# Moving the last head group's rows in five chunk-sized groups instead of eight pairs, with a turned ring and new orders

## Chip, cores and metric

One core of one Trainium2 chip runs the kernel. The metric is the device time of one execution in microseconds (us).

## The reference

Four layers in a row over x of 2048 tokens and 448 features: attention, MLP, attention, MLP (the same weights twice), each with a layernorm without weights and a residual. Attention is local and dilated: 16 heads of 28, and a token looks at 8 keys, 2 tokens apart.

```python
    def _A_ref(x, wqkv, wo):
        B, S, D = x.shape
        H = 16; Dh = D // H
        W, dil = 8, 2
        ...
        logits = jnp.einsum("bhsd,bhswd->bhsw", q, kg) * scale
        logits = jnp.where(mask[None, None, :, :], logits, -1e9)
        attn = _softmax(logits, axis=-1)
        o = jnp.einsum("bhsw,bhswd->bhsd", attn, vg)
        return (lambda x, *d: x.transpose(*d))(o, 0, 2, 1, 3).reshape(B, S, D) @ wo

    def _B_ref(x, w_gate, w_up, w_down):
        g = jnp.einsum("bsd,df->bsf", x, w_gate)
        u = jnp.einsum("bsd,df->bsf", x, w_up)
        h = g * u
        return jnp.einsum("bsf,fd->bsd", h, w_down)
    ...
    x = x + _A_ref(_layernorm(x, axis=-1), A_wqkv, A_wo)
    x = x + _B_ref(_layernorm(x, axis=-1), B_w_gate, B_w_up, B_w_down)
    x = x + _A_ref(_layernorm(x, axis=-1), A_wqkv, A_wo)
    x = x + _B_ref(_layernorm(x, axis=-1), B_w_gate, B_w_up, B_w_down)
```

## The kernel before, in words

**Blocks and chunks.** The 2048 tokens are 16 blocks of 128 (0 to 15). The layers are numbered 0 to 3; 0 and 2 are attention, 1 and 3 the MLP. They are worked off in chunks that interleave: the chunks of layer 2 are 512 tokens each, those of layer 3 are 256, 512, 512, 512 and 256 tokens, that is blocks 0 to 1, 2 to 5, 6 to 9, 10 to 13 and 14 to 15.

**Matmuls.** Nearly all whole matmuls are issued by a helper at L352, in pairs on the upper and lower half of TensorE's rows. The same products can be issued at L355 as four strips of 32 columns, which stand between the small matmuls of an attention burst (scores at L837, probabilities times values, AV, at L872) and fill TensorE there.

**Attention.** Queries and keys are cast out of PSUM (qk, L714, on ScalarE or VectorE as the order says); the keys' rows that hold the values are written to a DRAM tensor vt (L723), and come back transposed as v_sb (L734). In this way AV needs a transposed load. The results are copied to O_sb (L886, L890). `norm` divides them by the sums of the probabilities: a shuffle (L900), Ln and Exp on ScalarE (L901, L902) and a VectorE multiply (L913), which writes the bf16 values to the ring oT. The ring holds 8 blocks, 1024 tokens (`HALF`), so a multiply whose tokens cross token 1024 is cut in two there.

**Output projection.** `y_blocks` makes the projection of two blocks. A head has 28 rows in a group of 32, so 4 rows in each group are free. In layer 2 (`FOLD`) the last four heads' rows are moved into these free rows, and 7 pairs of matmuls do instead of 8. That takes five moves for each two blocks on SyncE's DMA queue (SP): four of them (`mv`, by the table `PADS`) wait for the norms of the two blocks; the fifth (`mw`) waits for the four and shifts what is left of the odd block to the other half of the partitions. The matmuls of both blocks wait for the fifth. All five are plain DMAs of L445. The rows of the weights wo_g are moved in the same manner once (`wf`), after the last projection of layer 0.

**Order.** Nothing decides the order at run time. A table `ORDER` gives for each engine and for SP the numbers of the operations in their order, with burst entries that say which strips stand between which small matmuls; `BANKS` gives the PSUM banks. Waits on semaphores are put in from the dependences. An instruction that waits holds up all that stands behind it on its engine, and a DMA issue that waits holds up all DMAs behind it on SP.

**MLP.** For 14 slices of 128 features, gate and up matmuls (a unit, 14 matmuls for each), ScalarE's copy g_sb (L979), VectorE's multiply hT (L982), then the down projection with WD. The last two blocks are done by full-width matmuls (L994) with the addition at L998. All other projections are added to x_sb on VectorE (L943).

Of the kernel before, what the change touches and what calls it, by code (L numbers as in the profile page):

```python
# [7 lines left out]
S = 2048  # L8
D = 448
# [24 lines left out]
FOLD = {0: 16, 2: 0}  # L34
PADS = ((0, 64, 4, 14, 0), (1, 96, 4, 15, 0), (2, 80, 3, 14, 16), (3, 112, 3, 15, 16))
# [61 lines left out]
def grp_nc(g):  # L97
# [283 lines left out]
def build(nc, A_x, A_wqkv, A_wo, B_w_gate, B_w_up, B_w_down, out):  # L381
# [513 lines left out]
    def norm(li, g, qb, os_, prio):  # L895
# [15 lines left out]
        for a, z in zip(cut, cut[1:]):  # L911
            def fn(E, a=a, z=z):
                return E.tensor_tensor(oT[:, :, a % HALF:a % HALF + z - a], O[:, :, a - tok:z - tok], R_sb[:, rs, 0:w].rearrange("p (h n) -> p h n", h=4)[:, :, a - tok:z - tok], ALU.mult)  # L913
# [211 lines left out]
```

## Time and profile before

| what | value |
|---|---|
| median of 3 runs | 383.45 us (383.18 to 383.95) |
| profiled execution | 383.47 us, its span 381.7 us |
| granted TensorE clock | 1.0 |
| TensorE (PE) busy | 373.9 us, 98% |
| VectorE (DVE) busy | 288.1 us, 75% |
| ScalarE (ACT) busy | 198.0 us, 52% |
| GpSimd (POOL) busy | 7.8 us, 2% |

A row of the timeline gives start and length in us, the engine, the line, the operation, what it writes and reads, how many instructions are grouped, and in brackets the idle time before it with the releaser that the semaphores suggest. SPq is SyncE's DMA queue: the length there is that of the issue, not of the transfer. A row of the waits gives total us, times, and the longest one. A row of the windows gives the length of the stretch, then busy time and instructions of PE, PEld (weight load), DVE, ACT and POOL, the granted clock, the DMA share and GB/s.

### The profile page before, as it was taken

What the parts mean: (1) busy time and instruction counts of PE and PEld (TensorE: products, weight loads), DVE (VectorE), ACT (ScalarE), POOL (GpSimd) and SP (SyncE); (2) the same over time, 40 slices, a digit from 0 to 9 for tenths busy, and PEclk for the clock granted to TensorE, in tenths of its full rate; (3) what the DMA queues carried; (4) which work ended last, traced back from release to release, by engine and by line L of the source; (5) the groups of instructions that cost most, each with busy time, mean ns of one, the idle gap of its engine ahead of it and who ended that gap; (6) DMA issues with size and microseconds to landing.
All of it is one profiled execution on the core that took longest, in us unless ns stands there. A gap on an engine that the chain in (4) does not pass through costs nothing.

```text
span 381.7 us, 14424 instructions
## 1 busy us (share of the span) xinstructions
PE 373.9 (98%) x6388; PEld 209.8 (55%) x6388; DVE 288.1 (75%) x649; ACT 198.0 (52%) x379; POOL 7.8 (2%) x36
## 2 busy tenths in 40 slices
PE   7999999999999999999999999999989999999997
PEld 3645577654554445444676666555555544444864
DVE  7988999989759794968568977758887878266423
ACT  5798896766516355245645326628745633034410
POOL 7000000000000000000000000000000000000000
PEclk9999999999999999999999999999999999999999
DMA  7665543500130215332102221630124001502003
GB/s 262 165 158 147 96 127 81 97 7 3 26 78 16 43 25 72 43 43 44 34 18 27 45 50 29 106 47 6 25 43 76 9 19 29 122 17 47 2 2 120
DMA packets 56209, 22.97 MB, mean 60 GB/s; under 512 B 45812, under 2 KB 56132, under 8 KB 56148
## 3 DMA queue, kind: packets, MB, share of 16 engines
q1 hardware_dynamic: 56004, 22.00, 27.5%
q8 instruction: 50, 0.82, 0.9%
q14 instruction: 11, 0.09, 0.1%
q10 hardware_dynamic: 144, 0.06, 0.1%
HBM read 8.59 MB, written 2.71 MB: 30 GB/s over the span
## 4 chain that ended last, share of the span: by engine, by line
PE 91%; DVE 4%; ACT 2%; DMA 1%; issue 1%; SPq 0%; DVEq 0%
PE ps L352 82%; PE ps L355 4%; PE ps L837 2%; PE ps L872 2%; PE ps L994 1%; ACT qk L714 1%; DMA v_sb<-vt 1%; DVE xn_sb L604 1%; DVE st L583 1%; DMA x_sb<-in_A_x_dram 1%; DVE v_sb L806 0%; DVE WQK L522 0%; DVE hT L982 0%; DVE Qz L825 0%; DVE xnTa L628 0%
## 5 line engine op out<-in xcount | busy, mean ns | idle before, releaser
L352 PE MATMUL ps<-xnTb,WGU 64*128 64x512 bf16 (+1 forms) x1890 | 171.2, 332 | 0.3 <-DVE qk L714 0.3
L352 PEld LDWEIGHTS ps<-xnTb,WGU 64*128 64x128 bf16 x1890 | 92.3, 94 | 70.6 <-issue 1.6
L979 ACT ACTIVATE g_sb<-ps 128x512 bf16<-128x512 f32 (+1 forms) x140 | 69.3, 510 | 83.9 <-PE ps L352 72.0
L982 DVE TENSOR_TENSOR hT<-g_sb,ps 128x512 bf16<-128x512 bf16 (+1 forms) x140 | 78.0, 574 | 36.3 <-ACT g_sb L979 35.5
L352 PE MATMUL ps<-WD,hT 64*128 64x448 bf16 x794 | 81.3, 349 | 0.0
L352 PEld LDWEIGHTS ps<-WD,hT 64*128 64x128 bf16 x794 | 38.3, 94 | 33.3 <-ACT E_sb L847 0.4
L943 DVE TENSOR_TENSOR x_sb<-x_sb,ps 128x448 bf16<-128x448 bf16 x62 | 37.1, 613 | 21.6 <-PE ps L352 21.3
L352 PE MATMUL ps<-xnTa,WQK 64*128 64x512 bf16 (+1 forms) x490 | 51.8, 352 | 0.3 <-DVE WQK L522 0.2
L847 ACT ACTIVATE E_sb<-ps,shift_sb 128x1024 bf16<-128x1024 f32 (+1 forms) x36 | 37.5, 1072 | 12.0 <-PE ps L837 11.9
L583 DVE BATCH_NORM_STATS2 st<-x_sb 128x6 f32<-128x448 bf16 x64 | 38.3, 613 | 1.0 <-DMA x_sb<-in_A_x_dram 0.8
L604 DVE TENSOR_SCALAR xn_sb<-x_sb,mv,rstd 128x512 bf16<-128x512 bf16 (+1 forms) x64 | 35.4, 574 | 2.5 <-ACT rstd L588 2.0
L352 PEld LDWEIGHTS ps<-xnTa,WQK 64*128 64x128 bf16 x490 | 23.0, 94 | 20.7 <-DVE O_sb L890 0.4
L714 ACT ACTIVATE qk<-ps 128x1024 bf16<-128x1024 f32 (+1 forms) x29 | 26.6, 931 | 11.4 <-PE ps L352 6.3
L901 ACT ACTIVATE R_sb<-R_sb 128x480 f32<-128x480 f32 (+1 forms) x34 | 20.4, 604 | 17.2 <-DVE R_sb L900 17.0
L854 DVE TENSOR_TENSOR E_sb<-E_sb,MK 128x1024 bf16<-128x1024 bf16 (+1 forms) x36 | 23.5, 656 | 6.6 <-ACT E_sb L847 6.6
L352 PE MATMUL ps<-wo_g,oT 64*128 64x448 bf16 x236 | 27.1, 349 | 1.1 <-DVE hT L982 1.1
L913 DVE TENSOR_TENSOR oT<-O_sb,R_sb 128x480 bf16<-128x480 f32 (+3 forms) x36 | 21.9, 626 | 3.8 <-ACT R_sb L902 3.6
L352 PE MATMUL ps<-WV,xnTa 64*128 64x336 bf16 (+3 forms) x248 | 23.2, 304 | 0.5 <-DVE O_sb L890 0.5
L900 DVE STREAM_SHUFFLE R_sb<-O_sb 128x480 f32<-128x480 f32 (+1 forms) x34 | 23.1, 692 | 0.0
L586 ACT ACTIVATE lnv<-mv,eps_sb 128x2 f32<-128x2 f32 (+2 forms) x31 | 9.0, 295 | 25.9 <-DVE mv L585 24.0
L902 ACT ACTIVATE R_sb<-R_sb 128x480 f32<-128x480 f32 (+1 forms) x34 | 20.0, 607 | 0.3
L886 ACT ACTIVATE O_sb<-ps 128x512 f32<-128x512 f32 (+1 forms) x20 | 10.9, 570 | 15.8 <-PE ps L872 15.8
(66 smaller groups left out, 223.8 us busy)
## 6 DMA issues: line engine op xcount, KB each, us to landing
out_dram<-x_sb SPq DMA_DIRECT2D x15, 112.0 KB, 1.8
x_sb<-in_A_x_dram SPq DMA_DIRECT2D x3, 448.0 KB, 5.3
hT<-in_A_wqkv_dram SPq DMA_DIRECT2D x4, 224.0 KB, 4.4
WGU<-in_B_w_gate_dram SPq DMA_DIRECT2D x4, 224.0 KB, 3.9
WGU<-in_B_w_up_dram SPq DMA_DIRECT2D x4, 224.0 KB, 4.5
WD<-in_B_w_down_dram SPq DMA_DIRECT2D x2, 448.0 KB, 3.8
WGU<-in_B_w_gate_dram SPq DMA_DIRECT2D x2, 336.0 KB, 4.5
WGU<-in_B_w_up_dram SPq DMA_DIRECT2D x2, 336.0 KB, 4.8
```

Source lines behind the costliest of these rows:

```text
L352: return lambda E: E.matmul(out(), lhs(), rhs(), start=start, stop=stop)
L583: sc.add("dve", one(lambda E, B=B: E.bn_stats(st6[:, B, :], x_sb[:, B, :]), ("bn", li, B)), 525.0, deps=[("x", li - 1, B)] + ([("xn", li - ...
L604: sc.add("dve", one(lambda E, B=B, dst=dst, src=src: E.tensor_scalar(dst, src, mv[:, B, 0:1], rstd[:, B:B + 1], ALU.subtract, ALU.mult), ( ...
L714: return E.activation(dst, src, ACT.Copy) if hasattr(E, "activation") else E.tensor_copy(dst, src)
L847: return E.activation(E_sb[:, slot, 2 * hp:2 * hp + 2, 0:w], ps[:, b0:b0 + 2, 0:w], ACT.Exp, bias=shift_sb[:, 0:1], scale=SCALE)
L854: return E.tensor_tensor(e, e, MK[:, kind, 0:nc].unsqueeze(1).unsqueeze(1).to_broadcast([128, 2, w // nc, nc]), ALU.min)
L900: sc.add("dve", one(lambda E: E.stream_shuffle(R_sb[:, rs, 0:w], O_sb[:, os_, 0:w], [DH] * 32), ("Rs", li, qb)), dve_est(w) + 20.0, deps=[ ...
L901: sc.add("act", one(lambda E: E.activation(R_sb[:, rs, 0:w], R_sb[:, rs, 0:w], ACT.Ln), ("Rl", li, qb)), act_est(w, False), deps=[("Rs", l ...
L913: return E.tensor_tensor(oT[:, :, a % HALF:a % HALF + z - a], O[:, :, a - tok:z - tok], R_sb[:, rs, 0:w].rearrange("p (h n) -> p h n", h=4 ...
L943: sc.add("dve", one(lambda E: E.tensor_tensor(x_sb[:, B, :], x_sb[:, B, :], ps[:, bk[w], 0:D], ALU.add), ("x", li, B)), dve_est(D), deps=[ ...
L979: sc.add("act", one(lambda E, gs=gs, bk=bk: E.activation(g_sb[:, gs, 0:nt], ps[:, bk[0], 0:nt], ACT.Copy), ("G", li, j, fc)), act_est(nt), ...
L982: sc.add("dve", one(lambda E, gs=gs, bk=bk, fc=fc: E.tensor_tensor(hT[:, fc, hs, 0:nt], g_sb[:, gs, 0:nt], ps[:, bk[1], 0:nt], ALU.mult), ...
```

## The change

The moves are made once for each chunk of layer 3's MLP: `GROUPS` names the first blocks 0, 2, 6, 10 and 14. The four `mv` of a group wait for the norms of all its 2 or 4 blocks, and each projection of the group waits for the group's one `mw`. That makes 25 moves instead of 40; those of four blocks are 512 tokens wide instead of 256. For a group to lie in one piece in the ring, the ring is turned by 256 tokens: block B stands at place (B + 2) % 8 instead of B % 8, and norms are cut at tokens 768 and 1792 instead of 1024. The orders and banks of all engines are written anew.

```diff
+GROUPS = (0, 2, 6, 10, 14)
...
-        cut = [tok] + [HALF] * (tok < HALF < tok + nq) + [tok + nq]
+        cut = [tok] + [e for e in range(HALF - 256, S, HALF) if tok < e < tok + nq] + [tok + nq]
...
-        nd = []
-        for qb in range(NQB):
-            _, _, tok, nq = qb_info(qb)
-            if tok < 128 * (B + 2) and tok + nq > 128 * B:
-                nd.append(("N", li, qb))
+        def norms(b0, b1):
+            return [("N", li, qb) for qb in range(NQB) if qb_info(qb)[2] < 128 * b1 and qb_info(qb)[2] + qb_info(qb)[3] > 128 * b0]
+        nd = norms(B, B + 2)
         fold = B >= FOLD[li]
         if fold:
-            a = 128 * (B % 8)
-            for j, row, m, _, _ in PADS:
-                plain_dma("sp", oT[32 * j + DH:32 * j + 32, 0:m, a:a + 256], oT[row:row + 4 * m, 3, a:a + 256], ("mv", li, B, j), ...
-            plain_dma("sp", oT[64:128, 3, a + 128:a + 256], oT[0:64, 3, a + 128:a + 256], ("mw", li, B), ...
-            nd = nd + [("mw", li, B)]
+            G = max(g for g in GROUPS if g <= B)
+            n = min([g for g in GROUPS if g > B] + [NBLK]) - G
+            if B == G:
+                a = 128 * ((B + 2) % 8)
+                for j, row, m, _, _ in PADS:
+                    plain_dma("sp", oT[32 * j + DH:32 * j + 32, 0:m, a:a + 128 * n], oT[row:row + 4 * m, 3, a:a + 128 * n], ("mv", li, B, j), ...
+                odd = [oT[lo:lo + 64, 3, a:a + 128 * n].rearrange("p (b w) -> p b w", w=256)[:, :, 128:256] for lo in (64, 0)]
+                plain_dma("sp", odd[0], odd[1], ("mw", li, B), ...
+            nd = nd + [("mw", li, G)]
...
 ORDER = {
     "sp": (
...
-        "841 847 763 765 772 776 917 819 777 915 919 921 1016 1018 816 817 815 814 935 820 821 934 822 938 939 936 818 823 937 940 945 944 950 949 1076 1074 973 "
+        "763 841 765 845 819 776 820 772 915 777 917 919 921 944 1013 1011 939 821 936 940 938 937 815 934 822 816 823 817 935 814 818 1164 945 950 949 1071 "
```

What the new orders do is seen at three places.

**SP, the moves of blocks 6 to 9.** Here `oT<-oT 4x4x…` and `4x3x…` are the four `mv`, `64x128` or `64x2x128` the `mw`, and `vt<-qk` the writes of keys and values of the last chunk of layer 2. Before, from the `mw` of blocks 6 and 7 on:

```order
L445 DMA oT<-oT 64x128
L723 DMA vt<-qk 4x4x512 x5
L445 DMA oT<-oT 4x4x256
L445 DMA oT<-oT 4x3x256
L445 DMA oT<-oT 4x4x256
L445 DMA oT<-oT 4x3x256
L734 DMA_TRANSPOSE v_sb<-vt 128x128
L723 DMA vt<-qk 4x4x512 x2
L445 DMA oT<-oT 64x128
```

After:

```order
L723 DMA vt<-qk 4x4x512 x4
L445 DMA oT<-oT 4x4x512
L445 DMA oT<-oT 4x3x512 x2
L445 DMA oT<-oT 4x4x512
L723 DMA vt<-qk 4x4x512 x3
L445 DMA oT<-oT 64x2x128
L734 DMA_TRANSPOSE v_sb<-vt 128x128 x3
```

Ten moves in two sets have become five in one; between `mv` and `mw` stand three writes of vt, where a transposed load and two writes stood.

**TensorE, the projections of blocks 6 to 9.** Matmuls with wo_g and oT are the projection, WV those of the values, xnTb with WGU gate and up. Before, behind the score burst of 17 small rows that the projection's first eight matmuls precede:

```order
L352 MATMUL ps<-wo_g,oT 128x448 x6
L352 MATMUL ps<-WV,xnTa 128x336 x6
L352 MATMUL ps<-xnTb,WGU 128x512 x14
L352 MATMUL ps<-WV,xnTa 128x336 x14
L352 MATMUL ps<-wo_g,oT 128x448 x8
L352 MATMUL ps<-WV,xnTa 128x336 x8
L352 MATMUL ps<-wo_g,oT 128x448 x6
```

After, from the end of the gate and up strips of the burst before (the score burst of 17 rows left out):

```order
L352 MATMUL ps<-xnTb,WGU 128x512 x20
L352 MATMUL ps<-WV,xnTa 128x336 x6
L352 MATMUL ps<-xnTb,WGU 128x512 x14
L352 MATMUL ps<-WV,xnTa 128x336 x22
...
L352 MATMUL ps<-wo_g,oT 128x448 x28
L352 MATMUL ps<-xnTb,WGU 128x512 x18
```

The projections of blocks 6 to 9 stand together, and all 28 matmuls of WV and a score burst stand ahead of them.

**SP, the transposed loads of the first bursts of layer 2.** `wo_g<-in_A_wo_dram` is a `wf`, which waits for the last projection of layer 0. Before:

```order
L723 DMA vt<-qk 4x4x512 x2
L734 DMA_TRANSPOSE v_sb<-vt 128x128 x2
L607 DMA_TRANSPOSE xnTa<-xn_sb 128x4x128
L445 DMA wo_g<-in_A_wo_dram 4x1792
L734 DMA_TRANSPOSE v_sb<-vt 128x128
L607 DMA_TRANSPOSE xnTa<-xn_sb 128x4x128 x3
```

After:

```order
L445 DMA wo_g<-in_A_wo_dram 4x1792
L734 DMA_TRANSPOSE v_sb<-vt 128x128
L445 DMA wo_g<-in_A_wo_dram 4x1792
L734 DMA_TRANSPOSE v_sb<-vt 128x128
L607 DMA_TRANSPOSE xnTa<-xn_sb 128x4x128
L734 DMA_TRANSPOSE v_sb<-vt 128x128
```

All three loads stand behind a `wf` now, the last of them behind two and one transpose of xn_sb.

More of the change, by code (lines that the diff above doesn't have):

```diff
@@ L918, in y_blocks @@
         bk = Banks(2)
-        nd = []
-        for qb in range(NQB):
-            _, _, tok, nq = qb_info(qb)
-            if tok < 128 * (B + 2) and tok + nq > 128 * B:
-                nd.append(("N", li, qb))
+        def norms(b0, b1):
+            return [("N", li, qb) for qb in range(NQB) if qb_info(qb)[2] < 128 * b1 and qb_info(qb)[2] + qb_info(qb)[3] > 128 * b0]
+        nd = norms(B, B + 2)
         fold = B >= FOLD[li]
         if fold:
-            a = 128 * (B % 8)
-            for j, row, m, _, _ in PADS:
-                plain_dma("sp", oT[32 * j + DH:32 * j + 32, 0:m, a:a + 256], oT[row:row + 4 * m, 3, a:a + 256], ("mv", li, B, j), f"d_m{li}_{B}", deps=nd, prio=prio - 0.1)
-            plain_dma("sp", oT[64:128, 3, a + 128:a + 256], oT[0:64, 3, a + 128:a + 256], ("mw", li, B), f"d_m{li}_{B}", deps=[("mv", li, B, j) for j in range(4)], prio=prio - 0.1, mode=1)
-            nd = nd + [("mw", li, B)]
+            G = max(g for g in GROUPS if g <= B)
[3 more added lines that the diff above has]
+                for j, row, m, _, _ in PADS:
+                    plain_dma("sp", oT[32 * j + DH:32 * j + 32, 0:m, a:a + 128 * n], oT[row:row + 4 * m, 3, a:a + 128 * n], ("mv", li, B, j), f"d_m{li}_{B}", deps=norms(B, B + n), prio=prio - 0.1)
+                odd = [oT[lo:lo + 64, 3, a:a + 128 * n].rearrange("p (b w) -> p b w", w=256)[:, :, 128:256] for lo in (64, 0)]
+                plain_dma("sp", odd[0], odd[1], ("mw", li, B), f"d_m{li}_{B}", deps=[("mv", li, B, j) for j in range(4)], prio=prio - 0.1, mode=1)
+            nd = nd + [("mw", li, G)]
             if B == FOLD[li] and li == min(l for l in FOLD if FOLD[l] < NBLK):
```

6 lines of the change are left out of this document (3 added, 3 removed), and 129 rows, old and new, of tables (BANKS, ORDER).

## The prediction

> **What bounds the kernel now.** I read the page first (busy shares, the slices with the granted clock, the chain that ended last), then TensorE's waits, the timeline about each wait that the change can touch, and the windows for the stretch where VectorE is fullest.
>
> ```profile
> PE 373.9 (98%) x6388; PEld 209.8 (55%) x6388; DVE 288.1 (75%) x649; ACT 198.0 (52%) x379; POOL 7.8 (2%) x36
> PEclk9999999999999999999999999999999999999999
> PE 91%; DVE 4%; ACT 2%; DMA 1%; issue 1%; SPq 0%; DVEq 0%
> ```
>
> TensorE is busy for 373.9 of 381.7 us at full granted clock, and the chain runs through it for 91%. So the time is TensorE's work plus its gaps, 7.8 us. The matmul work does not change: the groups in the order of both kernels hold the same products, and where strips take the place of whole matmuls, four strips replace one. I therefore ask only which gaps close and which open. TensorE's waits, longest first:
>
> ```profile
> PE ps L514 <- DVE hT L475: 1.3, 1, 1.3
> PE ps L352 <- DVE hT L982: 1.1, 1, 1.1
> ...
> PE ps L872 <- DMA v_sb<-vt: 0.5, 1, 0.5
> PE ps L352 <- DVE O_sb L890: 0.5, 1, 0.5
> PE ps L352 <- DVE qk L714: 0.3, 1, 0.3
> ```
>
> The first belongs to the head, whose loads the change leaves alone. The second is the one that the moves can touch. About it, in this order: whole matmuls of L352 from 258 to 280 us by operand (minimum, median and maximum in ns, first and last start), SyncE's issues, VectorE, and the two TensorE rows about the wait:
>
> ```profile
> L352 PE MATMUL ps<-xnTb,WGU x104: 373/376/387, 258.2 to 275.7; 64*128 64x512 bf16 x104
> L352 PE MATMUL ps<-xnTa,WQK x28: 376/376/376, 261.2 to 264.0; 64*128 64x512 bf16 x28
> L352 PE MATMUL ps<-wo_g,oT x28: 346/349/361, 272.3 to 280.0; 64*128 64x448 bf16 x28
> L352 PE MATMUL ps<-WV,xnTa x28: 302/303/303, 274.0 to 279.5; 64*128 64x336 bf16 x28
> ```
>
> ```profile
> 269.97 2.69 SPq L445 DMA_DIRECT2D oT<-oT  x4
> 272.70 1.12 SPq L734 DMA_TRANSPOSE v_sb<-vt  x1
> 273.87 0.82 SPq L723 DMA_DIRECT2D vt<-qk  x2
> 274.73 0.54 SPq L445 DMA_DIRECT2D oT<-oT  x1
> ```
>
> ```profile
> 269.28 0.66 DVE L913 TENSOR_TENSOR oT<-O_sb,R_sb 128x480 bf16<-128x480 f32 x1
> 269.86 0.68 DVE L982 TENSOR_TENSOR hT<-g_sb,ps 128x512 bf16<-128x512 bf16 x1
> ```
>
> ```profile
> 275.95 1.16 PE L352 MATMUL ps<-WV,xnTa 64*128 64x336 bf16 x14
> ...
> 278.25 0.93 PE L352 MATMUL ps<-wo_g,oT 64*128 64x448 bf16 x8 [1.14 <-DVE hT L982]
> ```
>
> The wait at 278.25 is put down to a VectorE multiply, but that had ended before. What the output projection of blocks 8 and 9 still lacked is the last of its five moves, the shift issued at 274.73: 3.5 us from its issue to the matmul. The norm of those blocks ended at 269.28 + 0.66 = 269.94, and its four moves were issued right behind it.
>
> **The change, step by step.**
>
> *1. The wait at 278.25 goes.* Blocks 8 and 9 now share their moves with blocks 6 and 7, and both projections stand together. Whatever wait there is falls on the first: **−1.14 us**.
>
> *2. A wait at blocks 6 and 7 comes.* Their projection now needs the norm that blocks 8 and 9 needed. I measure from the end of the attention burst that made these values, 258.2, where whole matmuls set in again. TensorE reached this projection at 272.3, +14.1. The new order puts the 28 matmuls of WV ahead of it (14 in 1.16 us by the row at 275.95, the last 0.3 of it pipeline: about 2.0 for 28) and one burst of scores (some 0.4): it arrives at about +16.5. The norm ended at 269.94, +11.75. One multiply of the MLP fewer stands ahead of it on VectorE (0.68 us, as in the row at 269.86). The norm also needs ScalarE's reciprocal, which moves less, so I take 0.45 of it: +11.3. Then four moves of 2.69 in all, the last one's landing, and the shift. How long these take:
>
> ```profile
> 207.20 5.66 PE L352 MATMUL ps<-WD,hT 64*128 64x448 bf16 x58
> ...
> 216.37 1.33 DVE L913 TENSOR_TENSOR oT<-O_sb,R_sb 128x480 bf16<-128x480 f32 x2 [0.25 <-ACT R_sb L902]
> ...
> 221.00 2.55 SPq L445 DMA_DIRECT2D oT<-oT  x2
> ...
> 222.58 1.69 PE L352 MATMUL ps<-xnTb,WGU 64*128 64x256 bf16 x28
> ...
> 225.43 0.92 PE L352 MATMUL ps<-wo_g,oT 64*128 64x448 bf16 x7
> ```
>
> ```profile
> 263.48 4.49 SPq L445 DMA_DIRECT2D oT<-oT  x5
> ```
>
> The five of 263.48 take 4.49; without 2.69 for four and 0.54 for the shift, 1.26 passes until the last move has landed. The shift of blocks 4 and 5 was issued at 221.00 + 2.55 − 0.54 = 223.01, and its matmuls began unhindered at 225.43, so it takes at most 2.4. Norm to landing is then at most 2.69 + 1.26 + 2.4 = 6.4 us, and the landing at most +17.7. The wait lies between 0 (a shift of 1.2) and 1.2; with the late shift of 3.5 seen above it is 2.3. I take **+0.7**, near the normal shifts. The three writes of vt that SP issues between moves and shift (two took 0.82 us at 273.87) fit into the 1.26. The moves are twice as wide as any in the trace; writes of vt, of 512 columns too, took 0.41 each to issue, less than a move's 0.67, so I add nothing for the width, up to 0.3 in the range.
>
> *3. Blocks 4 and 5, 2 and 3.* They too now wait for one group, whose last norm ended at 216.37 + 1.33 = 217.70, +10.5 from its burst's end at 207.20. The first projection of the group is now that of blocks 4 and 5. It was reached at 225.43, +18.2; the order now has two gate and up units of the MLP behind it that stood ahead (the 28 matmuls at 222.58, 1.5 us without their pipeline), and the projection of blocks 2 and 3 (7 pairs of the kind at 225.43, about 1.3), so it comes at about +15.4. One O_sb copy and several residual additions and statistics no longer stand between burst and norm; part of them stand before, as backlog, so I take +9.7. Landing at most 16.1: a wait of 0 to 0.7, **+0.1**. With the norm where it was, it would be 1.5. The groups of blocks 10 to 13 and 14 to 15 have over 20 us of room: nothing.
>
> *4. The wait for a transposed load.*
>
> ```profile
> 158.83 0.42 SPq L445 DMA_DIRECT2D wo_g<-in_A_wo_dram  x1
> 159.30 2.36 SPq L734 DMA_TRANSPOSE v_sb<-vt  x1
> ...
> 162.82 0.25 PE L872 MATMUL ps<-E_sb,v_sb 64*32 64x64 bf16 x16 [0.53 <-DMA v_sb<-vt]
> ```
>
> This load stood on SP behind a weight piece that waits for the last projection of layer 0. By the pairs that the order now has ahead of it, that projection comes about 2.5 us earlier on TensorE, and the load is wanted last of three instead of second. A second weight piece, 0.42, and one transpose stand ahead. I take **−0.53**; the bounds are −0.53 and +0.5, a transpose of about 1.2 that meets the full wait again.
>
> *5. The head.*
>
> ```profile
> 10.83 0.64 DVE L522 COPY WQK<-hT 128x448 bf16<-128x448 bf16 x3
> 11.52 0.72 PE L352 MATMUL ps<-xnTa,WQK 64*128 64x256 bf16 x10 [0.24 <-DVE WQK L522]
> ```
>
> One of VectorE's five copies of WQK passes to ScalarE, and one small copy leaves GpSimd. The first projection of queries and keys waited 0.24 for the last of the three copies at 10.83. One copy fewer takes that wait away: **−0.2**, between −0.6 (all three copies' 0.64) and +0.6 (as much, if ScalarE's copy comes last).
>
> *6. VectorE where it is full.*
>
> ```profile
> 40.00:60.00 20.00, 19.17 (x463) 13.29 (x459) 19.49 (x47) 18.73 (x35) 0.00 (x0) 1.00 0.43 90
> ```
>
> ```profile
> L714 DVE CAST qk<-ps 128x1024 bf16<-128x1024 f32 x5 | 6.1, 1216 | 0.9 <-PE ps L352 0.9
> ```
>
> Between 40 and 60 us VectorE is busy for 19.49 and ScalarE for 18.73 of 20, and TensorE's two small waits of 0.5 and 0.3 lie there. Three of the casts of 1216 ns go from ScalarE to VectorE, against copies of O_sb the other way; the norms get two more instructions by their new cuts (under 0.3 each, behind which nothing waits). **+0.2**, between −0.4 and one uncovered cast, +1.2.
>
> *7. Nothing* for the 15 moves fewer on SP by themselves (some 10 us of issue at 2.69 / 4): what they free on SP counts only where a transfer ends a wait, in 1 to 4. Nothing for the tail, whose last matmuls keep their number, ± 0.2.
>
> **Sum:** −1.14 + 0.7 + 0.1 − 0.53 − 0.2 + 0.2 = −0.87. The profiled execution took 383.47 us, 381.7 of it span, practically the median of 383.45: **382.6 us**. By the bounds of single terms this case reaches from 381.6 to 383.6.
>
> **A rule against it.** The late shift at 274.73 came right behind two writes of vt; the new shift comes right behind three. The Trainium skill, "DMA: Bandwidth & Descriptors", on HWDGE ordering in its section on queues, says that a DMA's semaphore increment lands only after every earlier write of the same DMA engine, so a shift would wait for the writes to DRAM ahead of it. By that rule the shift is late each time, and the sum is that of rival A below. The 3.5 us here agree with it, in one case only, and no row tells it from another cause.
>
> **The rivals.**
>
> *A, the wait is only replaced.* The group's shift, like the late one, lands 3.5 us after its issue because writes of vt to DRAM stand ahead of it. Then step 2 costs 2.3 − 0.5 (a norm somewhat earlier) = 1.8 in place of 0.7: **383.7**. For it: the one late shift had such writes ahead. Against: the vt writes had 0.9 us of lead, and the shift outlasted them by far. Chance 0.2.
>
> *B, slower: the group waits for its last norm.* Moves that started with a pair's own norm now start with the group's last one, and that norm sits in a full VectorE queue. If both last norms come where they come now (+11.75, +10.5), landing is at +18.2 and +16.9, against projections at +16.5 and +15.4: 1.7 + 1.5 = 3.2 us of waits, against 1.67 removed in 1 and 4, and with 5 and 6 cancelling: **385.0**. It decides from the point at which the two waits together pass 1.7, that is, when the norms come within 0.7 us of their old places and the shift takes the full 2.4. A further VectorE cast ahead of a norm adds 1.2. For it: VectorE's busy slices; the fewer instructions ahead of a norm may come back as backlog. Against: norms and shift are bounded from above. Chance 0.26.
>
> *C, both waits go.* Shifts of under 2 us and norms a little earlier leave 0.1 of step 2, and the head gives 0.5: −1.14 − 0.53 + 0.1 − 0.5 + 0.1 = −2.0: **381.5**. Chance 0.14. That the change doesn't take place is excluded: the order shows 25 moves where 40 were.
>
> **How the numbers follow.** Forecast 0.4, A 0.2, B 0.26, C 0.14. About 0.2% is what a measurement of this kernel can tell from no change, here 0.77 us: below 382.68 is faster, above 384.22 slower. Of the forecast's 0.4 a little over two thirds, 0.28, lies below 382.68, the rest within; C is faster. A is within for 0.15 and adds 0.05 to slower; B is slower for 0.25. So faster 0.42, within 0.28, slower 0.3. The range leaves out the far half of C and of B: 381.1 to 385.3.
>
> **What would show it.** Right: no wait of over 0.3 us at the projection of blocks 8 and 9; one of 0.2 to 1.2 at that of blocks 6 and 7, with its norm near +11.3 from the burst's end; no wait of AV matmuls for v_sb near 160 us; TensorE's idle time at about 6.9 us. A shows as a shift of over 3 us between its issue and the matmul, B as two waits of projections, each with moves issued late behind a norm. Wrong altogether: new waits of the gate and up matmuls on hT or g_sb, or of scores on qk, between 40 and 100 us, of over 1 us, or a longer head.

## The result, and the profile after

The changed kernel takes 384.74 us (median of 11 runs, 383.87 to 385.45); the kernel before, in the same session, takes 383.18 us (median of 11, 381.50 to 384.18). The ratio is 1.0052, 95% interval 1.0035 to 1.0069: the change makes the kernel slower, by about 1.6 us, where the forecast was 0.9 us faster. The profiled execution took 384.43 us, 382.6 of it span, at granted clock 1.0 throughout. One execution of one kernel below took 781 us, twice as long as all others, and is left out of its median.

TensorE's row of the page:

```profile
PE 375.7 (98%) x6382; PEld 212.0 (55%) x6382; DVE 289.8 (76%) x652; ACT 195.6 (51%) x379; POOL 7.8 (2%) x35
```

Both waits that the prediction meant to lose are gone, as the rows below show: no wait at an output projection, none for v_sb. Idle time is 382.6 − 375.7 = 6.9 us, to the tenth what the prediction gave, but by chance: other waits have come. And still the span is 0.9 us longer: TensorE's *busy* time rose from 373.9 to 375.7, for the same products. The idle time of the page alone does not say where time is lost.

So I look at where the waits stand. The timeline of TensorE in the changed kernel, the rows with a wait behind the first 20 us (start, length, engine, line, operation, count, in brackets the idle time before):

```profile
22.04 0.32 PE L837 MATMUL ps<-Qz,qk 64*64 64x144 bf16 x8 [0.23 <-DVE xnTa L628]
22.78 0.82 PE L352 MATMUL ps<-xnTa,WQK 64*128 64x512 bf16 x6 [0.43 <-DVE WQK L530]
44.98 0.64 PE L837 MATMUL ps<-Qz,qk 64*64 64x128 bf16 x32 [0.31 <-ACT qk L714]
50.25 1.71 PE L352 MATMUL ps<-xnTb,WGU 64*128 64x256 bf16 x28 [0.99 <-DVE E_sb L854]
77.77 5.79 PE L352 MATMUL ps<-xnTb,WGU 64*128 64x512 bf16 x52 [0.79 <-DMA xnTb<-xn_sb]
```

All five stand ahead of 78 us, and there are no others over 0.2 us behind. The same stretch of the kernel before has two, and begins the last of these products earlier:

```profile
46.03 0.60 PE L352 MATMUL ps<-WV,xnTa 64*128 64x336 bf16 x6 [0.50 <-DVE O_sb L890]
49.35 1.70 PE L352 MATMUL ps<-xnTb,WGU 64*128 64x256 bf16 x28 [0.33 <-DVE qk L714]
75.54 4.70 PE L352 MATMUL ps<-xnTb,WGU 64*128 64x512 bf16 x42
```

The windows from 20 to 78 us, before and after (length, then busy time and instructions of PE, PEld, DVE, ACT, POOL):

```profile
20.00:78.00 58.00, 56.97 (x1256) 35.40 (x1254) 53.05 (x132) 47.63 (x82) 0.58 (x3) 1.00 0.50 113
```

```profile
20.00:78.00 58.00, 55.00 (x1242) 33.62 (x1239) 53.38 (x131) 46.35 (x80) 1.85 (x8) 1.00 0.54 110
```

TensorE is busy 1.97 us less there. That is about the loss, and it lies far ahead of the moves of layer 2, which begin at 180 us or later.

**A marker.** The first gate and up product of 512 columns in layer 1 (the row at 75.54 before, at 77.77 after) cuts both programs into equal parts: the matmuls that start from there on are the same in both orders, with four strips counted as one. Of the products of xnTb and WGU with 512 columns, for one, 1106 whole ones and 280 strips are left before, 1120 and 224 after, 1176 either way. So its start says what the front cost, and span minus start what the rest cost. Before: 75.54, and 381.7 − 75.54 = 306.2. After: 77.77, and 382.6 − 77.77 = 304.8. The front lost 2.23 us, the rest gained 1.33, together the 0.9 of the spans.

**What is late in the front.** Both new waits are for layer 1's normalised values, which SyncE's transposes (L607) bring to xnTb. SyncE's queue, before and after (start and length of the issue, count):

```profile
43.71 2.76 SPq L607 DMA_TRANSPOSE xnTb<-xn_sb  x2
...
67.70 0.47 SPq L723 DMA_DIRECT2D vt<-qk  x1
68.94 1.22 SPq L607 DMA_TRANSPOSE xnTb<-xn_sb  x1
70.21 0.47 SPq L723 DMA_DIRECT2D vt<-qk  x1
70.73 1.22 SPq L607 DMA_TRANSPOSE xnTb<-xn_sb  x1
```

```profile
44.09 2.69 SPq L607 DMA_TRANSPOSE xnTb<-xn_sb  x2
...
69.11 2.47 SPq L723 DMA_DIRECT2D vt<-qk  x4
71.63 1.22 SPq L607 DMA_TRANSPOSE xnTb<-xn_sb  x1
72.90 0.47 SPq L723 DMA_DIRECT2D vt<-qk  x1
73.41 1.22 SPq L607 DMA_TRANSPOSE xnTb<-xn_sb  x1
```

The time from issue to landing stands in the DMA view of a window that holds one issue (count, last figure in us). The second transpose of the pair near 44 us and the one at 70.73, before:

```profile
xnTb<-xn_sb SPq DMA_TRANSPOSE x1, 3.7
```

```profile
xnTb<-xn_sb SPq DMA_TRANSPOSE x1, 2.9
```

The same two after, the second of them issued at 73.41:

```profile
xnTb<-xn_sb SPq DMA_TRANSPOSE x1, 4.5
```

```profile
xnTb<-xn_sb SPq DMA_TRANSPOSE x1, 4.3
```

So the first pair is complete some 1.1 us later, though issued only 0.3 to 0.4 us later: 44.09 + 2.69 − 1.27 (one issue) + 4.5 = 50.0, when TensorE starts again at 50.25. The wait is put down to a VectorE write of E_sb, which ended at 50.03, as good as together with the landing, so this row alone does not tell them apart. In other runs of the new front the view names the landing itself, and the product starts 0.25 us behind it as here (with the transposes alone moved, below, the landing is at 50.37 and the product at 50.62). So I take it that the landing ends the wait. The last transpose is issued 2.7 us later and is 1.4 us longer under way: 73.41 + 4.3 = 77.7, and the product begins at 77.77. VectorE's write of the values that it fetches, before and after:

```profile
69.43 0.73 DVE L604 TENSOR_SCALAR xn_sb<-x_sb,mv,rstd 128x896 bf16<-128x896 bf16 x1
```

```profile
71.43 0.72 DVE L604 TENSOR_SCALAR xn_sb<-x_sb,mv,rstd 128x896 bf16<-128x896 bf16 x1
```

The values are ready at 70.16 before and 72.15 after, 2.0 us later; the other 0.7 of the 2.7 is SyncE's queue, where four writes of vt now stand ahead of these two transposes instead of one. In the kernel before the last transpose landed at 70.73 + 2.9 = 73.6, and its product began at 75.54: there was a margin of 1.9 us, which shows in no wait.

### The profile page after: what moved, and what is told of

Read it like the earlier page. It is cut to its first block, busy times and chain, and to the rows that moved or that the text cites. A ratio compares the mean times of both kernels' runs of the same rounds, so it can differ in the third digit from the quotient of the medians.

```text
span 382.6 us, 14404 instructions
## 1 busy us (share of the span) xinstructions
PE 375.7 (98%) x6382; PEld 212.0 (55%) x6382; DVE 289.8 (76%) x652; ACT 195.6 (51%) x379; POOL 7.8 (2%) x35
## 4 chain that ended last, share of the span: by engine, by line
PE 89%; DVE 6%; DMA 2%; ACT 1%; issue 1%; DVEq 0%
PE ps L352 79%; PE ps L355 3%; DMA xnTb<-xn_sb 2%; PE ps L514 2%; PE ps L837 2%; PE ps L872 2%; PE ps L996 1%; DVE R_sb L900 1%; DVE xn_sb L604 1%; DVE hT L984 1%; DVE x_sb L945 1%; PE ps L618 1%; ACT qk L714 1%; DVE st L583 0%; DVE oT L913 0%
## 5 line engine op out<-in xcount | busy, mean ns | idle before, releaser
L352 PE MATMUL ps<-xnTb,WGU 64*128 64x512 bf16 (+1 forms) x1904 | 173.4, 332 | 1.9 <-DVE E_sb L854 1.0
L714 ACT ACTIVATE qk<-ps 128x1024 bf16<-128x1024 f32 (+1 forms) x27 | 23.9, 910 | 6.2 <-PE ps L352 6.0
L352 PE MATMUL ps<-wo_g,oT 64*128 64x448 bf16 x230 | 26.0, 349 | 0.1
L913 DVE TENSOR_TENSOR oT<-O_sb,R_sb 128x480 bf16<-128x480 f32 (+5 forms) x38 | 22.0, 599 | 1.9 <-ACT R_sb L902 1.9
L872 PEld LDWEIGHTS ps<-E_sb,v_sb 64*32 64x32 bf16 x1088 | 13.8, 90 | 7.1 <-issue 2.8
L872 PE MATMUL ps<-E_sb,v_sb 64*32 64x64 bf16 (+1 forms) x1088 | 17.2, 191 | 0.0
```

The lines of the kernel that those rows point to most:

```text
L352: return lambda E: E.matmul(out(), lhs(), rhs(), start=start, stop=stop)
L714: return E.activation(dst, src, ACT.Copy) if hasattr(E, "activation") else E.tensor_copy(dst, src)
L872: parts[eb // 2].append((lambda E, b=b, c=c, o=o, vw=vw, eb=eb, eo=eo: E.matmul(ps[32 * b:32 * b + 32, bk[c], o:o + nc], vw, E_sb[64 * c:6 ...
L913: return E.tensor_tensor(oT[:, :, (a + 256) % HALF:(a + 256) % HALF + z - a], O[:, :, a - tok:z - tok], R_sb[:, rs, 0:w].rearrange("p (h n ...
```

## The experiments

Three ideas were to be told apart. **L**: the two waits of the kernel before that the prediction counted as gains come from transfers that land late in some of its executions only. **F**: the loss is made by the new order of the front, in the waits for xnTb, and the grouped moves cost nothing. **B**, the rival: the groups, or what was written anew around them, cost the time behind 148 us. In the expectations of the second to the fourth run F is called S and B is called M; in the first, "rival F" is only the denial of L. The exchange kernels join the order and banks of one kernel up to some place on TensorE to those of the other behind it, on all engines, with each operation once. Where one line more stands at the head of such a kernel, its line numbers are higher by one or two.

### The kernel before, once more

No edit.

> The kernel before, once more, for a second profile. Theory L (the 1.14 us wait at blocks 8 and 9 and the 0.53 us wait for the transposed load come from transfers that land late in some executions only): the ratio to before is 1.000 within 0.003, and its profile lacks one of the two waits, or has another late transfer; single times spread over 381.5 to 384.2. Rival F (the waits are fixed by the order): both waits are there again, 1.0 to 1.3 and 0.4 to 0.7 us.

Measured: 383.14 us (381.44 to 384.04), ratio 1.0006 (0.9989 to 1.0023); the profiled execution 381.81, span 380.1. It has neither wait. The shift of blocks 8 and 9, and the projection that lacked it:

```profile
273.91 0.54 SPq L445 DMA_DIRECT2D oT<-oT  x1
...
276.12 0.92 PE L352 MATMUL ps<-wo_g,oT 64*128 64x448 bf16 x8
```

The projection starts 2.2 us after the shift's issue, with no idle time ahead, where it took 3.5 us in the first profile; the same order, the same two writes of vt ahead. L holds, as far as two profiles can show it: the 1.67 us of waits belong to the first execution and do not come each time. This execution is one of the fastest of its kernel; by the median of 383.14, late landings of some kind may still be common. The Trainium skill, "DMA: Bandwidth & Descriptors", in its section "Queues, rings and completion order" on HWDGE ordering, says that a DMA's semaphore follows all earlier writes of the same DMA engine; by the prediction's reading of that rule the shift would be late each time, and this trace does not bear it out. Its marker:

```profile
75.39 4.91 PE L352 MATMUL ps<-xnTb,WGU 64*128 64x512 bf16 x44
```

Front 75.39, rest 380.1 − 75.39 = 304.7: 1.5 less than in the first profile, and as much as in the changed kernel (304.8).

### Front of the kernel before to 100 us, rest of the changed one

Against the changed kernel, TensorE's order in the front, one place of many:

```diff
-405 580 406 310 307 387 313 388 319 304 322
+405 580 406 387 307 310 388 313 319 322 304
```

> Orders and banks of before up to about 100 us (164 entries of TensorE's order and what they need), behind them orders, banks and grouped moves of the changed kernel. Theory S (the loss lies in the new orders of the first 100 us, where the changed kernel's profile falls 2.3 us behind; the grouped moves and the rest gain 0.7 to 1.9): 381.0 to 382.2, ratio to before 0.994 to 0.999. Rival M (grouped moves or the later orders cost the time): like the changed kernel, ratio 1.003 to 1.007.

Measured: 388.58 us, ratio 1.0146 (1.0122 to 1.0170), at a granted clock of 0.991 to 0.996.

```profile
118.01 4.26 PE L353 MATMUL ps<-xnTb,WGU 64*128 64x512 bf16 x24 [4.22 <-DMA xnTb<-xn_sb]
```

At the seam the two orders have not done the same work, and TensorE waits 4.22 us for xnTb. The time is far outside the expectation, and as a total the run says nothing on the change. Its front does: no wait over 0.5 us at 50 or 77 us, marker at 75.26.

### The mirror: front of the changed kernel to 100 us

Against the kernel before, the same place the other way round:

```diff
-405 580 406 387 307 310 388 313 319 322 304
+405 580 406 310 307 387 313 388 319 304 322
```

> The mirror: orders and banks of the changed kernel up to about 100 us, behind them orders, banks and paired moves of before. Theory S: ratio to before 1.004 to 1.008, with TensorE's waits for xnTb or E_sb between 45 and 80 us. Rival M: ratio 0.998 to 1.002.

Measured: 389.93 us, ratio 1.0183 (1.0160 to 1.0206), at a granted clock of 0.996 to 1.0. Again the seam rules, the expectation is missed, and the total is inconclusive:

```profile
120.23 4.28 PE L353 MATMUL ps<-xnTb,WGU 64*128 64x512 bf16 x38 [3.33 <-DMA xnTb<-xn_sb]
```

In its front stand waits of 1.18 us at 50.13 and 0.40 at 77.25, and the marker is at 77.25, with the kernel before behind it.

### Pairs of moves in the new order

```diff
-GROUPS = (0, 2, 6, 10, 14)
+GROUPS = (0, 2, 4, 6, 8, 10, 12, 14)
 ORDER = {
     "sp": (
...
-1069 973 972 974 971 1135 975 1137 1139 1141
+1076 1074 973 972 974 971 1000 1001 1002 1003 1140 975 1004 1142 1144 1146
```

The second pair's five moves of each group of four blocks are put right behind the first pair's; all else is the changed kernel.

> The changed kernel with moves for each pair of blocks again (40 moves; the second pair's five stand right behind the first pair's), all else as in the changed kernel, ring turned. Theory S, by which the grouping itself is worth little once the projections stand together: ratio to the changed kernel within 0.2%, so 1.003 to 1.007 to before, the projections of blocks 6 to 9 starting without a wait or with one under 0.7 us. Rival M (moves by groups cost): ratio to before below 1.002.

Measured: 385.66 us, ratio 1.0076 (1.0058 to 1.0094), against 1.0052 for the changed kernel. The front is as slow (waits of 1.07 and 0.69 us at 49.87 and 77.28), and the projections of blocks 6 to 9 wait, since the queue now issues five moves more ahead of them:

```profile
277.55 2.64 PE L354 MATMUL ps<-wo_g,oT 64*128 64x448 bf16 x26 [1.34 <-DVE E_sb L856]
```

The expectation (a wait under 0.7 us, a time within 0.2% of the changed kernel's) is missed on the slow side. In the new order the groups save time, by these two profiles: 306.3 us behind the marker here (383.6 − 77.28), 304.8 with them. The intervals of the two ratios overlap, so the times alone do not show it. Nothing says that the groups are what costs.

### Front of the kernel before to 148 us

At this place the two orders have done nearly the same work. Against the changed kernel, the last operations of the front on TensorE (behind them all is as there):

```diff
-795+796*720/2/4 652 721 769 653 724 770
+795+796*720/2/5 721 770 652 653 724
```

> The orders and banks of the kernel before for all that it runs up to about 148 us, and behind that those of the changed kernel with its five groups of moves and its turned ring. At this place both orders have done nearly the same work, so that no wait like the 4.22 us at the seam of the earlier exchange at 100 us should stand there. Theory F (the loss is made ahead of 100 us, by shares of the normalised values that land later in the new order, and the grouped moves neither gain nor lose more than some tenths): TensorE waits under 0.6 us behind the seam, none at 50 and 77 us of the size of 0.99 and 0.79, and the time is that of the kernel before in its executions without late landings, 381.3 to 383.0, ratio 0.995 to 1.001. Theory B (the groups and what stands around them cost the 1.5 us): 384.0 to 385.5, ratio 1.003 to 1.007.

Measured: 383.00 us (median of 11), ratio 1.0003 (0.9984 to 1.0022). The time is that of F; for a profile the kernel was run once more.

> The kernel of the exchange at 148 us once more (the front of the kernel before, the rest of the changed one), for a profile, since the one taken of it was disturbed (779 us). Theory F: TensorE's waits at 46 and 49 us as in the kernel before (0.5 and 0.3 us), none of 0.99 at 50 and none of 0.79 at 77; behind 148 us no wait over 0.6 us, and a profiled time of 381.3 to 383.0. Theory B: the lag behind the kernel before grows by over 1 us behind 148 us.

Measured: 382.56 us (381.53 to 383.86), ratio 0.9981 (0.9965 to 0.9998); the profiled execution 383.68, span 381.9.

```profile
75.72 4.49 PE L353 MATMUL ps<-xnTb,WGU 64*128 64x512 bf16 x40 [0.52 <-DMA xnTb<-xn_sb]
...
255.67 1.69 PE L353 MATMUL ps<-xnTa,WQK 64*128 64x512 bf16 x14 [1.12 <-DMA xnTa<-xn_sb]
```

The front is the old one again (75.72), the rest 306.2. Of that, 1.12 us is a late landing at 255.67, which the changed kernel's own profile does not have: the expectation's "no wait over 0.6 behind 148 us" and its profiled time of at most 383.0 missed, since landings are late there too, now and then. With it taken off, the rest is 305.1. A wait of 0.52 us stands at the marker too, which the kernel before has in neither profile: the last transpose was issued at 71.73 here, 1 us later than there, and took 3.9 us, with the same order on SyncE's queue up to it. Groups, turned ring and new orders behind 148 us together are worth between +0.03% and −0.19%, by the two runs; B falls.

### The mirror at 147 us

```diff
-795+796*720/2/5 721 770 652 724 653
+795+796*720/2/4 652 721 769 653 724 770
```

> The mirror: the orders and banks of the changed kernel up to about 147 us, behind that those of the kernel before with its eight pairs of moves. Theory F: the waits of 1.0 us at 50 and 0.8 at 77 us stand as in the changed kernel, and the time is 384.0 to 386.5, ratio 1.003 to 1.009, as slow as the changed kernel or slower, since the pairs' moves can still land late behind it. Theory B: 382.5 to 383.7, ratio 0.999 to 1.002.

Measured: 385.57 us (384.70 to 386.53), ratio 1.0074 (1.0048 to 1.0099). As F has it:

```profile
50.28 1.70 PE L353 MATMUL ps<-xnTb,WGU 64*128 64x256 bf16 x28 [0.99 <-DVE E_sb L855]
77.64 5.79 PE L353 MATMUL ps<-xnTb,WGU 64*128 64x512 bf16 x52 [0.63 <-DMA xnTb<-xn_sb]
```

With the kernel before behind it, moves in pairs and all, the new front costs as much as in the changed kernel. The rest is 382.6 − 77.64 = 305.0.

### One burst ahead of the gate and up products

```diff
-406 310 307 387 313 388 319
+406 387 310 307 313 388 319
 BANKS = (
...
-307:23 310:45 313:67
-387:01
+307:23 310:67 313:01
+387:45
```

(All banks behind this place are renamed in the same manner.)

> The changed kernel, with one burst of probability times V (16 + 16 matmuls of 32x64, 0.33 us) put ahead of the first two gate and up products of layer 1, as it stands in the kernel before, and the PSUM banks renamed from there on so that each still follows a bank that is free. Theory F: the wait of 0.99 us at 50.25 in the changed kernel falls to 0.3 to 0.8 us, and the time by about as much, to a ratio of 1.003 to 1.005. Rival: what is behind the burst waits for the same landing, so that the wait is just moved and the time stays within 0.1 us of the changed kernel's 384.7 (ratio 1.005).

Measured: 385.51 us (384.27 to 386.70), ratio 1.0069 (1.0047 to 1.0092): no gain, which is the rival's side.

```profile
50.12 0.28 PE L872 MATMUL ps<-E_sb,v_sb 64*32 64x64 bf16 x4 [0.46 <-issue]
50.96 2.47 PE L352 MATMUL ps<-xnTb,WGU 64*128 64x256 bf16 x42 [0.56 <-DVE qk L714]
```

The wait is cut in two, 0.46 + 0.56, and as long as ever. Two things hold the product here. The second transpose of the pair took 4.8 us and landed near 50.5, half a us later than in the changed kernel. And the product has bank pair 67 now instead of 45, which VectorE's cast of qk frees only at 50.81:

```profile
50.13 0.68 DVE L714 CAST qk<-ps 128x512 bf16<-128x512 f32 x1
```

The product starts 0.15 us behind that cast, as it does at 49.35 in the kernel before, where the cast ended at 49.21. So the landing alone does not decide in this run, and what the place of the burst is worth by itself stays untold. At the marker the wait has grown to 1.10 us.

### The same, and the last two transposes earlier on SyncE

The edit above, and:

```diff
-441 443 595 594 597 592 445 591 447 596
+441 443 595 594 592 445 447 597 591 596
```

445 and 447 are the transposes issued at 71.63 and 73.41 in the changed kernel; 591 to 597 are writes of vt. The expectation speaks of three and one writes; those that the edit moves behind the two transposes are 597, and 591, which stood between them.

> The edit of the run before, and on SyncE's queue the last two transposes of layer 1's first half put ahead of three and one writes of vt that stand ahead of them in the changed kernel. Theory F: the last transpose is issued some 1.2 us earlier than its 73.1 us, lands by 76.5, and the wait of 0.79 us at 77.77 goes; the time falls by 0.8 us more than by the edit before, to a ratio of 1.000 to 1.003. Rival: the transpose takes longer to land beside other transfers (4.3 us from issue to semaphore in the changed kernel against 2.9 in the one before), or the delayed writes of vt make a wait at the transposes of V behind them; then the time stays within 0.2 us of the edit before.

Measured: 383.99 us (383.31 to 385.56), ratio 1.0036 (1.0017 to 1.0055), 1.5 us less than the run before on the same chip.

```profile
77.17 3.19 PE L352 MATMUL ps<-xnTb,WGU 64*128 64x512 bf16 x28
```

The time is a little above the expectation's 1.000 to 1.003. No wait stands at the marker, and its start is 77.17, where it was 78.44 with the burst alone; the wait at 51 us is still there (1.27). The last transposes landed 3.0 us after their issue here:

```profile
xnTb<-xn_sb SPq DMA_TRANSPOSE x2, 3.0
```

The earlier place in the queue brings the last issue forward by only 0.5 us against the changed kernel, since its values are ready late; that it is 1.3 us less under way than in the changed kernel is most of what the wait lost.

### The transposes alone

The changed kernel with this last diff alone.

> The changed kernel with one edit on SyncE's queue alone: the last two transposes of layer 1's first half ahead of three and one writes of vt. The burst of probability times V stays where the changed kernel has it. If the issue of the last transpose, 2.7 us later than in the kernel before, made the wait of 0.79 us at 77.77, that wait goes, the one of 0.99 us at 50.25 stays, and the time falls by 0.7 to 1.5 us against the changed kernel: a ratio of 1.001 to 1.0035. If the gain of the last run came from its two edits together, the time stays at 384.3 to 385.0 (1.004 to 1.006).

Measured: 384.80 us (383.45 to 386.61), ratio 1.0042 (1.0023 to 1.0061).

```profile
50.62 1.60 PE L352 MATMUL ps<-xnTb,WGU 64*128 64x256 bf16 x26 [1.27 <-DMA xnTb<-xn_sb]
```

In its profile (383.78 us) the marker has no wait and starts at 77.25, 0.52 us earlier than in the changed kernel, and not 0.8, since the wait at 50 us has grown by 0.28: this time its transpose took

```profile
xnTb<-xn_sb SPq DMA_TRANSPOSE x1, 4.8
```

The median moved by no more than its interval, and lies above the expected 1.001 to 1.0035, in the range that was given for "the two edits together". That the wait at the marker goes with these transposes is what this profile and the one before show (the next run has one of 0.48 us there all the same); that the time falls with it is shown by the run before and not by this one.

### Weight transfers behind the first two transposes

```diff
-303 301 367 368 370 514 364 516 517 365 369 515 366 97 98 520
+303 301 97 98 367 368 370 514 364 516 517 365 369 515 366 520
```

and the diff of the transposes. 303 and 301 are the first pair of transposes, 97 and 98 the two weight transfers.

> The edit of the run before, and two weight transfers of the MLP (16 large packets each) put right behind the first two transposes of layer 1, ahead of eleven writes of vt (35 packets each). Theory Q: the second transpose lands 4.5 to 4.8 us after its issue in the new order because of the writes of vt issued right behind it; then it lands here 3.0 to 3.7 us after, the wait of 0.99 us at 50.25 falls under 0.4, and the time falls by 0.6 to 0.9 us more, to a ratio of 0.999 to 1.001. Rival: the landing does not depend on what is issued behind, it stays at 4.3 to 4.8 us, and the time stays as in the run before, or rises by some tenths since the writes of vt come 0.9 us later.

Measured: 385.05 us (383.35 to 386.29), ratio 1.0048 (1.0028 to 1.0069). The profiled execution lost 1.5 us against the run before ahead of 13 us (waits of 0.75, 0.60 and 0.55 us, one of them for a load of WV), so only the distances inside it count. SyncE's issue of the pair, and TensorE's product:

```profile
45.72 2.77 SPq L607 DMA_TRANSPOSE xnTb<-xn_sb  x2
```

```profile
51.52 1.70 PE L352 MATMUL ps<-xnTb,WGU 64*128 64x256 bf16 x28 [0.64 <-DMA xnTb<-xn_sb]
```

The wait is halved, not gone. From the pair's first issue to the product 5.8 us pass (51.52 − 45.72), where it is 6.2 in the changed kernel (50.25 − 44.09) and 5.6 in the kernel before (49.35 − 43.71). The second transpose took 4.1 us and the first 4.9, where they take 4.5 and 3.1 in the changed kernel. So the second is neither at Q's 3.0 to 3.7 nor at the rival's 4.3 to 4.8, and the time did not fall. At the marker TensorE waits 0.48 us, though the last two transposes are moved here too. The run doesn't settle what Q asks.

### Front of the kernel before to 66 us

Against the changed kernel, the last operations of the front:

```diff
-310 307 387 313 388 319 304 322
+387 307 310 388 313 319 322 304
```

> The orders of the kernel before up to about 66 us, behind that those of the changed kernel, so that of the new front only the stretch from 66 to 148 us is left. At the first gate and up product of 512 columns in layer 1 the work still to do is the same in all these kernels; it starts at 75.4 to 75.7 us with the front of the kernel before and at 77.2 to 78.8 with the new one. If the loss ahead of it is made in both places (0.65 us more wait at 50 us and some tenths at 22 and 45, then the later last transpose), it starts at 75.9 to 76.6 here, with no wait over 0.5 at 50 and one of 0.3 to 0.9 ahead of it, and the time is at a ratio of 1.000 to 1.003. If nearly all of it is made ahead of 66 us, it starts by 75.8 without a wait, ratio 0.997 to 1.000; if nearly all is made behind, it starts at 77 or later, ratio 1.004 to 1.006.

Measured: 383.58 us (382.31 to 385.49), ratio 1.0016 (0.9997 to 1.0034).

```profile
76.60 5.79 PE L353 MATMUL ps<-xnTb,WGU 64*128 64x512 bf16 x52 [0.36 <-DMA xnTb<-xn_sb]
```

The loss is made in both places. The marker starts at 76.60, about halfway from 75.54 to 77.77, and the time lies between those of the two kernels, as expected. SyncE's queue has the order of the changed kernel from its start to its end in this run, and still TensorE waits only 0.33 us at 49.36, as in the kernel before: it is not the order on SyncE's queue by itself, with its writes of vt behind the pair, that makes the first pair late. What is left of the front's loss here is the last transpose: issued at 71.9 us behind the writes of vt, it took

```profile
xnTb<-xn_sb SPq DMA_TRANSPOSE x1, 4.6
```

Together, by marker and time:

| kernel | marker starts | rest | ratio to before |
|---|---|---|---|
| before, two profiles | 75.54, 75.39 | 306.2, 304.7 | 1 |
| old front to 148 us (second run's profile) | 75.72 | 306.2 | 1.0003, 0.9981 |
| old front to 66 us | 76.60 | 304.6 | 1.0016 |
| changed, burst and transposes | 77.17 | 304.4 | 1.0036 |
| changed, transposes | 77.25 | 304.7 | 1.0042 |
| changed, pairs of moves | 77.28 | 306.3 | 1.0076 |
| changed | 77.77 | 304.8 | 1.0052 |
| new front to 147 us | 77.64 | 305.0 | 1.0074 |
| changed, burst ahead | 78.44 | 304.7 | 1.0069 |
| changed, weights behind transposes | 78.76 | 305.6 | 1.0048 |

From the old front to the new one the time rises with the marker, though not in step with it from row to row. The rest is 304.4 to 305.0 in every profile without a wait over 0.5 us behind the marker, with the old orders and with the new ones; those above have one or more (1.14 and 0.53, 1.12, 1.34, and 0.97 us). No version beats the kernel before by more than the 0.2% that can be told; the old front to 148 us with the groups behind comes nearest.

## Why the prediction was wrong

**The step that failed is 6**, and with it the silence of the sum on all that follows up to 78 us. Step 6 priced the stretch from 40 to 60 us at +0.2 with a bound of +1.2, as casts of qk on VectorE; from 20 to 40 and from 60 to 78 us the sum has no term. Up to the marker, 2.2 to 2.4 us were lost (77.77 against 75.54 and 75.39). At the first gate and up product of layer 1 it is 0.9 (50.25 against 49.35), or 1.2 with the burst of 0.33 us that the kernel before has ahead of it and the changed one behind; the other 1.0 or so comes between there and the marker. VectorE's busy time from 20 to 78 us is hardly changed (53.05 to 53.38). What TensorE waits for are the transposed values: the pair of transposes that is complete 1.1 us later, and the last one, issued 2.7 us later and longer under way. The waits in TensorE's rows, 0.23 + 0.43 + 0.31 + 0.99 + 0.79 = 2.75 against 0.50 + 0.33 = 0.83, are 1.92 of the 2.2. The prediction had read the new order on SP at the moves and at the loads of v_sb, where a wait was to go, and not at these transposes, of which the last had no wait before; step 7 let SP count in steps 1 to 4 alone. Of the 2.7 us of the last issue, 2.0 are VectorE's later write of the values; how much of that is the delay at 50 us handed on, and how much the new order on VectorE, no run separates.

**Steps 1 and 4** are right for the changed kernel: both waits are gone. But 1.67 us of them was counted as a gain on the kernel before, which waits so only in some executions. The profiled time of 383.47 near the median made them look like the rule; between its executions, 381.5 to 384.2 us, lie 2.7 us. The "rule against it", by which the writes of vt ahead make the shift late each time, fell with the second profile.

**Steps 2 and 3** expected waits of 0.7 and 0.1 us at the groups' first projections. There are none. The end of the burst, the last norm, the moves of blocks 6 to 9, their shift and the projection in the changed kernel:

```profile
259.85 3.19 PE L352 MATMUL ps<-xnTb,WGU 64*128 64x512 bf16 x28
...
269.40 0.65 DVE L913 TENSOR_TENSOR oT<-O_sb,R_sb 128x480 bf16<-128x480 f32 x1
...
270.07 2.71 SPq L445 DMA_DIRECT2D oT<-oT  x4
274.40 0.70 SPq L445 DMA_DIRECT2D oT<-oT  x1
276.51 2.83 PE L352 MATMUL ps<-wo_g,oT 64*128 64x448 bf16 x28
```

The norm ended at 270.05, +10.2 from the burst's end at 259.85, and not at +11.3; the projection came at +16.7, close to the +16.5 worked out. Between norm and projection lie 6.5 us, a little more than the 6.4 that step 2 gave as the most that moves and shift take, so nothing waits. Rival A (a late shift behind three writes of vt) did not come: the projection starts 2.1 us after the shift's issue. The double width cost nothing that shows. Rival B, which ended slower, named the right sign and nearly the right time, 385.0, but by luck: no projection waits for its group's last norm. It is also luck that the measured 384.74 lies in the range, which reaches so far up for B's sake.

**Step 5**: the wait of 0.24 at the first queries and keys is gone, as said; two small ones at 22 us, 0.23 and 0.43, came in its place. **Step 7** foresaw no change in the tail, and none shows: the rest behind the marker is as long with the old tail as with the new one.

The terms behind the marker were forecast as −1.14 + 0.7 + 0.1 − 0.53 = −0.87. The first two profiles have −1.33 there, and the medians 1.56 − 2.23 = −0.7. Measured by itself, with the old front, it is +0.23 and −0.54 us (383.00 against 382.77, 382.56 against 383.10). So the gain of that part is smaller than forecast if there is one, and its sign is not shown; the front, which the sum put at −0.2 + 0.2, decided.

**Why the same transfer lands late in one case and not in another** is not shown by any edit, but the traces point at something that the experiments did not look for. In the DMA view of a window, the queue q8 that the profile calls "instruction" carries single large packets (0.02 MB, 50 in a run). The share is that of 16 engines. The late shift of the kernel before (274.7 to 278.2), and the same shift in its second profile (273.9 to 276.1):

```profile
q1 hardware_dynamic: 248, 0.08, 12.0%
q8 instruction: 1, 0.02, 2.5%
```

```profile
q1 hardware_dynamic: 120, 0.05, 12.9%
```

The last transpose in the kernel before (70.7 to 73.0, landing at 73.6; the next such packet starts at 73.0) and in the changed kernel (73.4 to 77.7):

```profile
q1 hardware_dynamic: 1386, 0.35, 77.5%
```

```profile
q1 hardware_dynamic: 1438, 0.36, 84.5%
q8 instruction: 1, 0.02, 1.9%
```

The late ones have such a packet beside them; the timely ones have none, or one that comes near their end. In the changed kernel it takes 1.9% of 16 engines in 4.3 us, that is 1.3 us of one engine, and the transpose is 1.4 us longer under way than in the kernel before. The first pair fits: the packet starts at 46.3 in the kernel before, where the transposes take 4.6 and 3.7 us, and at 47.8 in the changed one, behind the landing of the first (3.1) and beside the second (4.5). Over 13 profiles, the traces give the landing of 60 transposes to xnTb ahead of 80 us. The 18 without such a packet took 2.9 to 3.2 us, and all but one of the 37 that took 3.7 or more had one. Five had one that started 2.3 us or more behind the issue, and took 2.9 to 3.1 all the same. No run moves such a packet, so this remains a reading of the traces; what sets the time at which they start was not tried either.

## What to carry to other kernels

When an order is written anew, go through every transfer that something waits for, also those that had no wait: each has a margin, and the margin is spent without a trace in the waits of before. Take a second profile of the kernel before pricing a wait as a gain; a wait that ends with a landing may be there in one execution and not in the next. When the same transfer takes longer in one profile than in another, look in the DMA view at what the other queues carried beside it. To place a loss, find an instruction with the same work left in both kernels and compare its start: idle time alone missed 1.8 us here.

## What the hardware showed

- One and the same transpose, of the same values, took 2.9 us from issue to landing in both profiles of the kernel before, 3.9 in another kernel with the same orders up to there (the old front to 148 us), and 4.3 in the changed kernel. The longer ones had a large packet of the instruction queue beside them.
- A shift between partitions of 16 KB let its reader start 2.2 us after its issue in one execution and held it for 3.5 us in another of the same kernel, again with such a packet beside the late one alone.
- In the profile, TensorE's busy time is not the same for the same matmuls: 375.7 us in the changed kernel, 374.3 with burst and transposes moved, 6382 matmul records in both.
